# Attention followed by a max-out MoE on one core: the second product by Strassen's scheme in blocks of 512 tokens

## The chip, the core and the metric

The kernel runs on one core of one Trainium2 chip, alone. The metric is the device time of one execution in microseconds (us), lower is better. Before the change: 363.46 us, median of 3 runs (362.85 to 363.61).

## What is computed

Eight batches, eight heads, 1152 keys of 64 elements; the queries are averaged in pairs, so each head has 576 queries. The heads' outputs side by side are 4608 tokens `x` of 512 elements, which go through a two-branch max-out layer:

```
q_pool = q.reshape(B, H, S // 2, 2, D).mean(axis=3)
attn   = softmax(q_pool @ k.T / sqrt(D))
x      = (attn @ v).transpose(0, 2, 1, 3).reshape(4608, 512)
out    = np.maximum(x @ w1, x @ w2) @ w_out          # w1, w2: 512 x 1024; w_out: 1024 x 512
```

The kernel uses max(h1, h2) = h2 + relu(h1 - h2): with `wd = w1 - w2` and `w21 = w2 @ w_out`, formed once, out = x @ w21 + relu(x @ wd) @ w_out. So a token costs a first product (512 x 1024) and a second product whose contraction is 512 + 1024 = 1536 long, in 12 chunks of 128.

## The kernel before, in words

Two heads are one of 32 pairs. Their scores lie as one stream of 336 groups of 512 columns; a group is one `S` in the order of TensorE (PE): `scores` (L678) writes it into one of the PSUM buffers `sps0..2` (three for the first 21 groups, then two), and ScalarE (ACT) takes the exponential from there into `et` (L685). `av_jobs` (the `a` units: L589, and L601 for the 64 rows left over) multiply `et` by `v`, VectorE (DVE) divides by the sums (L611, L615, L619), and `xT`, the transposed tokens, is made by DMA (`xtrans`) or PE (`xtrans_pe`). GpSimd (POOL) casts k, v and q (L457, L496, L490). DVE also transposes q in 32 x 32 squares (L546).

The first product is `h_pairs` (`H` units, L877; later `h_jobs`, `h`, L850), evacuated by DVE with a relu into `gT` (L887, L861). The second product is `p_pair` (`P`): two tiles of 128 tokens, all 512 output columns, 12 chunks; one DVE copy (L919) frees its two banks, and `store_pair` sends the tokens out. The last tokens go tile by tile (`p_job`, `p`, L940). Here, 15 pairs make 3840 tokens and 6 tiles the other 768. `P`, `H` and `S` units use half the PE array's rows per matmul, two matmuls side by side (`duo`); `a`, `h`, `p` units use all 128 rows. Each `duo` job goes through its chunks twice (`turn` 0 and 1, the row halves exchanged), and the first unit of turn 1 carries `fence=True`: it waits until the unit before it on the same banks is complete.

Nothing is scheduled at run time. `pe_order` is a fixed string: one letter for each unit, `S` for a score group and a digit for the PSUM bank that a job runs in; the lists `jobs_of` say which job comes next in a bank. `dve_order`, `act_order`, `pool_order` and `sp_order` do the same for the other queues. `Plan` derives the waits from keys read and written (`r`, `w`): an instruction waits for the last writer of every key that it reads, and for the last writer and all readers, stores too, of every key that it writes.

Of the kernel before, what the change touches and what calls it, by code (L numbers as in the profile page):

```python
# [6 lines left out]
FP32 = mybir.dt.float32  # L7
# [12 lines left out]
class Plan:  # L20
# [26 lines left out]
    def lane(self, o):  # L47
# [3 lines left out]
        if o["eng"] == "POOL":  # L51
            return {"kb": "k", "wd": "d"}.get(key[:2], key[0])
# [5 lines left out]
        return {"qt": "T", "w2": "W", "wo": "W", "gd": "G"}.get(key[:2], "Q")  # L58
# [234 lines left out]
def bass_funnel_attn__then__act_maxout2_kernel(  # L293
# [23 lines left out]
    RING = 1024  # L317
    assert D == 64 and S == NT * P and QU == NT and C == H * D and E == 512
# [13 lines left out]
    with outer:  # L332
# [23 lines left out]
        xT = sbuf([P, NC_, NTOK], BF16, "xT")  # L356
# [6 lines left out]
        w2b = xT[:, :, 512:1536]  # L363
        w2T = xT[:, :, 1536:2560].rearrange("p c (f x) -> p c f x", x=P)
        w2f = xT[:, :, 2560:4608].bitcast(FP32)
# [3 lines left out]
        osb = [osb2[:, s, :] for s in range(4)]  # L369

# [132 lines left out]
        def dve(fn, r, w):  # L503
            op("DVE", fn, r=r, w=w)
# [216 lines left out]
        def xtrans(i):  # L721
            b, ct = divmod(i, NHP)
            for j, z, n0, n in spots(b):
                n1 = n0 + n * (z - j)
                op("SP", lambda e, j=j, z=z, n=n, n0=n0, n1=n1: e.dma_start_transpose(
                    xT[:, ct, n0:n1].rearrange("p (j x) -> p j x", x=n),
# [3 lines left out]
        def xtrans_pe(i):  # L730
# [9 lines left out]
            def evac(m):  # L740
                mb = fb[m][:, :].bitcast(BF16)
                op("DVE", lambda e: e.tensor_copy(xT[:, ct, b * SQ:b * SQ + SQ], mb[:, 0:SQ]),  # L742
                   r=[f"f{m}"], w=xkeys(ct, b * SQ, b * SQ + SQ) + [f"f{m}"],
                   after=under(ct, b * SQ, b * SQ + SQ))
            return Job([unit(xneed(i, 0) + xneed(i, 1) + ["ident"], go)], evac)

        def xkeys(ct, n0, n1):
            return [f"xT.{ct}.{j}" for j in range(n0 // HP, n1 // HP)]
# [40 lines left out]
        ocount = [0]  # L789
# [52 lines left out]
        def h_jobs(nb, tail):  # L842
# [24 lines left out]
        def h_pairs(nb):  # L867
# [4 lines left out]
            for f0 in range(0, NF, 2):  # L872
                def part(ct, turn, f0=f0):
                    def pair(e, m):
                        for k in range(2):
# [3 lines left out]
                                xT[z, ct, n0:n1], start=(turn == 0 and ct == 0),  # L879
# [13 lines left out]
        def p_pair(lo):  # L893

            def part(j, turn):
                if j < NC_:
                    r = [f"w21{j}"] + xkeys(j, lo, lo + 2 * P)
                else:
                    r = [f"wo{j - NC_}"] + [f"gT.{g}.{j - NC_}" for g in gkeys(lo, lo + 2 * P)]

                def pair(e, m):
                    for k in range(2):
                        z = rows(turn ^ k)
                        n = lo + k * P
                        if j < NC_:
                            lhs, rhs = xT[z, j, n:n + P], w21[z, j, :]
                        else:
                            c = n % RING
                            lhs, rhs = gT[z, j - NC_, c:c + P], wo[z, j - NC_, :]
                        last = e.matmul(fb[m + k][:, :], lhs, rhs, start=(turn == 0 and j == 0),  # L910
                                        stop=(turn == 1 and j == NC_ + NF - 1))
                    return last
                return duo(r, pair, turn == 1 and j == 0)

            def evac(m):
                ocount[0] += ocount[0] % 2
                o = ocount[0] % 4
                ocount[0] += 2
                dve(lambda e: e.tensor_copy(  # L919
                    osb2[:, o:o + 2, :], wide[m // 2][:, :, :]), [f"f{m}", f"f{m + 1}"],  # L920
# [330 lines left out]
```

## Time and profile before

| | |
|---|---|
| median of 3 runs | 363.46 us |
| span of the profiled execution, first to last instruction | 361.7 us |
| PE / ACT / DVE / POOL busy | 355.0 / 313.3 / 243.1 / 124.5 us |
| granted PE clock, mean | 0.999 |
| first and last exponential start | 6.4 and 329.8 us |
| chain that ended last: PE / ACT | 93% / 5% |

The profile shows one execution. A matmul's row gives its duration from first to last element; two that follow each other overlap, so what counts is the distance of their starts. "x8" in a row of the timeline merges eight instructions in a row.

### The profile page before, as it was taken

To read this page: it belongs to the slowest core of one execution; us is meant where nothing else is said; L and a number is where in the kernel's file an instruction comes from. 1 tells how busy PE (TensorE), PEld (TensorE's weight loads), DVE (VectorE), ACT (ScalarE), POOL (GpSimd) and SP (SyncE) were. 2 spreads that over 40 slices of the span, in tenths; PEclk is the share of its full clock that TensorE was granted. 3 is DMA by queue.
4 is the path that set the end of the run, shared out by engine and by line. 5 is a ranking of instruction groups with operands and counts; after the bars stand their busy time and mean duration, and the time that the engine had idled before them with its cause. 6 is when DMAs were issued, how large, how long until landed. Compare 5 with 4: busy or idle time off the path is not lost.

```text
span 361.7 us, 13398 instructions
## 1 busy us (share of the span) xinstructions
PE 355.0 (98%) x5973; PEld 222.1 (61%) x5973; DVE 243.1 (67%) x528; ACT 313.3 (87%) x355; POOL 124.5 (34%) x111
## 2 busy tenths in 40 slices
PE   8899999999999999999999999999999999999996
PEld 6666655566564666657575666666666565656753
DVE  3676787877589777866876687595977747625411
ACT  5999989989999999998999999989999988994221
POOL 1248967333055324452242426261234440010000
PEclk9999999999999999999999999999999999999999
DMA  7999999999959998997999999998999560805215
GB/s 239 408 394 398 402 286 296 244 286 344 246 123 242 284 302 235 251 256 179 285 309 184 269 277 284 305 251 202 243 215 269 169 153 15 198 16 87 52 30 147
DMA packets 77789, 84.76 MB, mean 234 GB/s; under 512 B 50080, under 2 KB 50848, under 8 KB 77728
## 3 DMA queue, kind: packets, MB, share of 16 engines
q1 hardware_dynamic: 77168, 83.09, 87.6%
q8 instruction: 47, 0.77, 0.9%
q10 hardware_dynamic: 560, 0.79, 0.6%
q14 instruction: 14, 0.11, 0.1%
HBM read 62.91 MB, written 9.44 MB: 200 GB/s over the span
## 4 chain that ended last, share of the span: by engine, by line
PE 93%; ACT 5%; issue 0%; DVE 0%; DVEq 0%
PE sps L678 20%; PE sps L589 13%; PE sps L910 12%; PE fb L910 10%; PE sps L877 9%; PE fb L589 7%; PE fb L877 7%; ACT et L685 5%; PE sps L940 3%; PE sps L601 2%; PE fb L802 2%; PE fb L940 1%; PE sps L850 1%; PE fb L601 1%; PE fb L850 1%; PE fb L411 1%
## 5 line engine op out<-in xcount | busy, mean ns | idle before, releaser
L685 ACT ACTIVATE et<-sps 128x1024 bf16<-128x1024 f32 (+1 forms) x336 | 305.2, 1009 | 20.5 <-PE sps L678 19.3
L678 PE MATMUL sps<-qpT,kT 64*128 64x256 bf16 (+7 forms) x1162 | 119.8, 284 | 1.7 <-DVE qpT L536 0.7
L546 DVE STREAM_TRANSPOSE qpT<-qp 32x288 bf16<-32x288 bf16 x216 | 101.4, 469 | 4.5
L678 PEld LDWEIGHTS sps<-qpT,kT 64*128 64x128 bf16 x1162 | 47.3, 94 | 51.1 <-ACT et L685 19.9
L490 POOL TENSOR_TENSOR qp<-qraw 128x576 bf16<-128x576 f32 x30 | 42.2, 1406 | 83.1 <-DVE qpT L546 58.6
L496 POOL TENSOR_SCALAR vE<-vraw 128x1152 bf16<-128x1152 f32 x32 | 36.8, 1152 | 62.8 <-DMA vraw<-in_v_dram 48.1
L589 PE MATMUL sps<-vE,et 128*128 128x65 bf16 x1440 | 51.2, 193 | 0.6 <-issue 0.4
L589 PEld LDWEIGHTS sps<-vE,et 128*128 128x128 bf16 x1440 | 46.0, 97 | 6.9 <-issue 5.4
L457 POOL TENSOR_SCALAR kbf<-kraw 128x1152 bf16<-128x1152 f32 x31 | 35.6, 1151 | 42.2 <-DMA kraw<-in_k_dram 29.6
L877 PE MATMUL sps<-xT,wd 64*128 64x512 bf16 (+3 forms) x368 | 42.8, 326 | 0.1
L910 PE MATMUL sps<-wo,stage 64*128 64x512 bf16 x256 | 37.5, 377 | 0.0
L877 PE MATMUL fb<-xT,wd 64*128 64x512 bf16 (+3 forms) x272 | 33.0, 334 | 0.1
L887 DVE TENSOR_SCALAR stage<-sps 128x1024 bf16<-128x1024 f32 (+3 forms) x23 | 22.3, 969 | 15.4 <-PE sps L877 15.2
L910 PE MATMUL fb<-wo,stage 64*128 64x512 bf16 x224 | 32.5, 377 | 0.0
L589 PE MATMUL fb<-vE,et 128*128 128x65 bf16 x864 | 30.5, 193 | 0.0
L589 PEld LDWEIGHTS fb<-vE,et 128*128 128x128 bf16 x864 | 27.5, 97 | 4.2 <-issue 3.2
L887 DVE TENSOR_SCALAR stage<-fb 128x1024 bf16<-128x1024 f32 (+3 forms) x17 | 17.0, 999 | 10.4 <-PE fb L877 10.1
L877 PEld LDWEIGHTS sps<-xT,wd 64*128 64x128 bf16 x368 | 15.6, 94 | 12.0 <-DVE xT L742 0.8
L611 DVE RECIPROCAL rcs<-sps 128x5 f32<-128x5 f32 (+1 forms) x40 | 7.3, 183 | 19.4 <-PE sps L589 18.7
L919 DVE COPY stage<-sps 128x1024 f32<-128x1024 f32 x8 | 9.8, 1224 | 13.8 <-PE sps L910 13.8
L910 PE MATMUL sps<-w,xT 64*128 64x512 bf16 x128 | 18.6, 377 | 0.0
L910 PE MATMUL fb<-w,xT 64*128 64x512 bf16 x112 | 18.1, 377 | 0.0
(94 smaller groups left out, 286.3 us busy)
## 6 DMA issues: line engine op xcount, KB each, us to landing
vraw<-in_v_dram SPq DMA_DIRECT2D x32, 576.0 KB, 6.3
kraw<-in_k_dram SPq DMA_DIRECT2D x31, 576.0 KB, 6.4
qraw<-in_q_dram SPq DMA_DIRECT2D x31, 576.0 KB, 6.0
out_dram<-stage SPq DMA_DIRECT2D x21, 256.0 KB, 5.4
out_dram<-stage SPq DMA_DIRECT2D x23, 128.0 KB, 3.0
xT<-in_moe_w_dram SPq DMA_DIRECT2D x4, 512.0 KB, 10.7
stage<-in_moe_w_out_dram SPq DMA_DIRECT2D x4, 512.0 KB, 13.7
stage<-in_moe_w_dram SPq DMA_DIRECT2D x4, 512.0 KB, 13.4
```

The lines of the kernel that those rows point to most:

```text
L457: op("POOL", lambda g: g.tensor_scalar(kbf[s][:, :, :, :].rearrange("p t h d -> p h t d"), kraw[r][:, :, :, :], 1.0, 1.0, ALU.mult, ALU.mu ...
L490: op("POOL", lambda g: g.tensor_tensor(qpf[s][:, :, :], qraw[r][:, :, 0, :], qraw[r][:, :, 1, :], ALU.add), r=[f"qraw{r}"], w=[f"qp{s}.0", ...
L496: op("POOL", lambda g: g.tensor_scalar(vE[r][:, :, :, 0:D].rearrange("p t h d -> p h t d"), vraw[r][:, :, :, :], 1.0, 1.0, ALU.mult, ALU.m ...
L546: op("DVE", lambda e: e.transpose(view[dst:dst + 32, :, 32 * pb:32 * pb + 32], qpf[s][src:src + 32, :, 32 * db:32 * db + 32]), r=[f"qp{s}. ...
L589: last = e.matmul(fb[m][:, sb * 66:sb * 66 + 65], et[:, a:a + P], vE[vs][:, t, half, 0:65], start=(t == 0), stop=(t == NT - 1))
L601: last = e.matmul(fb[m][rows(half), NCH * 66:NCH * 66 + 65], et[:, a:a + NB], vE[vs][:, t, half, 0:65], start=(t == 0), stop=(t == NT - 1))
L678: last = e.matmul(sps[r][:, h, col:col + hi - lo], kT[i % 3][rows(h), t, :], qpT[i % 3][rows(h), lo:hi], start=True, stop=True)
L685: op("ACT", lambda e: e.activation(et2[:, :, c:c + z - a], sps[r][:, :, a - g * W:z - g * W], EXP, scale=scale), r=[f"s{r}"], w=keys + ([f ...
L877: last = e.matmul(fb[m + k][:, 0:size], wd[z, ct, (f0 + k) * P:(f0 + k + 1) * P], xT[z, ct, n0:n1], start=(turn == 0 and ct == 0), stop=(t ...
L887: dve(lambda e: e.tensor_scalar_max(gT[:, f0:f0 + 2, g0:g0 + size], wide[m // 2][:, :, 0:size], 0.0), [f"f{m}", f"f{m + 1}"], w + [f"f{m}" ...
L910: last = e.matmul(fb[m + k][:, :], lhs, rhs, start=(turn == 0 and j == 0), stop=(turn == 1 and j == NC_ + NF - 1))
L940: return e.matmul(fb[m][:, 0:c1 - c0], lhs, rhs[:, c0:c1], start=(j == 0), stop=(j == NC_ + NF - 1))
```

## The change

Blocks of 512 tokens replace the pairs of 256 in the second product. The block's tokens are split in two sets of tiles (`row` 0 and 1), the contraction in two halves (`k`) and the 512 output columns in two halves (`c`), and Strassen's scheme in Winograd's form makes the four results from 7 products instead of 8. Each product is 6 chunks x 2 tiles x 2 row halves, 24 matmuls of 256 columns; so 168 matmuls of 256 columns for 512 tokens, where two `P` had 96 of 512. A block has four jobs (`P0.0` to `P0.3`) of two, two, two and one products, each with its own fence and its own evacuation.

New operations: `t_sums`, four sums of weight blocks, made once on DVE in two parts each; `s_sums`, four sums of token blocks for each block, in two parts each (`at` 0: from `xT`, 512 elements a partition; `at` 1: from `gT`, 1024), all on POOL but the parts `at` 1 of sums 1 and 3, which are on DVE; and the evacuations `end1` to `end4`, one copy and six adds of PSUM and `part`, in place of two copies. `xT` becomes a ring of 2304 tokens. Eight blocks make 4096 tokens, the last 512 go as four `p` tiles, and the output buffer of a `p` tile follows from its number, no longer from a counter.

Letters behind the first 208 PE units, the lists of jobs and the orders of the other queues are new.

```diff
-        xT = sbuf([P, NC_, NTOK], BF16, "xT")
+        xT = sbuf([P, NC_, XRING], BF16, "xT")              # XRING = NTOK // 2
+        extra = sbuf([P, NC_ * XRING], BF16, "extra")
...
+        tw = extra[:, 0:4 * KT * HE].rearrange("p (n t e) -> p n t e", n=4, t=KT)
...
+        sx = [t.rearrange("p (t j x) -> p t j x", t=KT, j=2) for t in (
+            extra[:, 4 * KT * HE:5 * KT * HE], extra[:, 5 * KT * HE:6 * KT * HE], spare16[:, 0:KT * HE])]
...
-        def p_pair(lo):
...
-                return duo(r, pair, turn == 1 and j == 0)
-            def evac(m):
...
-                dve(lambda e: e.tensor_copy(
-                    osb2[:, o:o + 2, :], wide[m // 2][:, :, :]), [f"f{m}", f"f{m + 1}"],
-                    [f"osb{o}", f"osb{o + 1}", f"f{m}", f"f{m + 1}"])
-                store_pair(lo, o)
+        def t_sums(n, at):
...
+            op("DVE", lambda g: g.tensor_tensor(t(n), one, two, ALU.subtract),
+               r=r, w=[f"tw{n}.{at}"], after=[f"w2f{c}" for c in range(NC_)])
...
+        def s_sums(lo, n, at):
+            t0, t1 = ((0, 2), (2, KT))[at]
+            a11, a12, a21, a22 = ((0, 0), (0, 1), (1, 0), (1, 1))
+            one, two, alu, dst = ((a21, a22, ALU.add, 0), (0, a11, ALU.subtract, 1),
+                                  (a11, a21, ALU.subtract, 2), (a12, 1, ALU.subtract, 1))[n]
...
+                op("DVE" if at and n % 2 else "POOL", lambda g, js=js, view=view: g.tensor_tensor(
+                    sx[dst][:, t0:t1, js, :], view(one, v1), view(two, v2), alu),
+                    r=r1 + r2, w=[f"sx{dst}.{at}"], after=[f"w2f{NC_ - 1}", f"wof{NC_ - 1}"], fence=True)
...
+        def p_block(lo):
...
+                def pair(e, m):
+                    for t in ts:                                # two chunks a unit
+                        for k in range(2):
+                            z = rows(turn ^ k)
+                            lhs, rhs = left(a, k, t)[0], right(b, t)[0]
+                            last = e.matmul(
+                                fb[m + k][:, x * HE:x * HE + HE], lhs[z, :], rhs[z, :],
+                                start=opening and t == 0, stop=closing and t == KT - 1)
...
+            def end1(m):
+                dve(lambda e: e.tensor_copy(part[:, :, 0, :], bank(m, X0)), [f"f{m}", f"f{m + 1}"], ["p1"])
+                add(m, part[:, :, 1, :], part[:, :, 0, :], bank(m, X1), ["p1"], ["u2"], True)
+            def end2(m):
+                add(m, otile(0)[:, :, 0:HE], part[:, :, 0, :], bank(m, X0), ["p1"], ["osb0.0", "osb2.0"],
+                    after=["osb0", "osb2"])
+                add(m, part[:, :, 0, :], part[:, :, 1, :], bank(m, X1), ["u2"], ["p1", "u3"], True)
+            def end3(m):
+                add(m, part[:, :, 1, :], part[:, :, 1, :], bank(m, X0), ["u2"], ["u2"])
+                add(m, otile(1).rearrange("p j (n e) -> p j n e", n=2),
+                    part[:, :, 0:1, :].to_broadcast([P, 2, 2, HE]),
+                    wide[m // 2].rearrange("p j (n e) -> p j n e", n=2), ["u3"], ["osb1", "osb3"], True)
+            def end4(m):
+                add(m, otile(0)[:, :, HE:E], part[:, :, 1, :], bank(m, X0), ["u2"], ["osb0", "osb2"], True)
+                for j in range(2):
+                    store_pair(lo + 2 * j * P, 2 * j)
...
+            return [Job(stage_units(ps), end) for ps, end in (
+                (((X0, A11, B11), (X1, 1, 1)), end1),
+                (((X0, A12, B21), (X1, 2, 2)), end2),
+                (((X0, 0, 0), (X1, A22, 3)), end3),
+                (((X0, 1, B22),), end4))]
...
             def evac_part(m):
-                o = ocount[0] % 4
-                ocount[0] += 1
+                o = lo // P % 4
...
-            "0S67676SS6677S0000S6S0066S660S6666S000S006S666S60S0000SS1111S666S0000S000S066S66S0000SS11011S"
+            "767SS666S66S0000S00S600S60S000S7777SS66666S000S00S60S0060S666S666S6000S000S066S66S660S66S1000S6S1011"
```

Three places show how the orders moved. In the names, `sps` and `fb` are PSUM, `vE,et` marks an `a` unit, `qpT,kT` a score group, `xT,wd` an `H` or `h` unit; `extra` and `stage` hold the sums.

PE, about the middle of the program, two heads' `a` jobs. Before:

```order
L601 MATMUL sps<-vE,et 64x65 x18
L589 MATMUL sps<-vE,et 128x65 x18
L678 MATMUL sps<-qpT,kT 128x384 x2
L678 MATMUL sps<-qpT,kT 128x128 x2
L678 MATMUL sps<-qpT,kT 128x448 x2
L678 MATMUL sps<-qpT,kT 128x64 x2
L589 MATMUL sps<-vE,et 128x65 x54
```

And in the changed kernel:

```order
L599 MATMUL sps<-vE,et 128x65 x9
L688 MATMUL sps<-qpT,kT 128x384 x2
L688 MATMUL sps<-qpT,kT 128x128 x2
L599 MATMUL sps<-vE,et 128x65 x27
L688 MATMUL sps<-qpT,kT 128x448 x2
L688 MATMUL sps<-qpT,kT 128x64 x2
L611 MATMUL sps<-vE,et 64x65 x18
L688 MATMUL sps<-qpT,kT 128x512 x2
L599 MATMUL sps<-vE,et 128x65 x18
```

A job of `a` units stood in two runs between the score groups, and stands in four now. Over the whole order the `a` units stand in 75 runs before and 102 now; the places where one unit uses the array in another row or column split than the unit before it are 218 before and 270 now.

PE again, the block of 128 tokens in the first product, before (8 matmuls of turn 0, a score group, 8 of turn 1):

```order
L877 MATMUL sps<-xT,wd 128x128 x8
L678 MATMUL sps<-qpT,kT 128x320 x2
L678 MATMUL sps<-qpT,kT 128x192 x2
L910 MATMUL fb<-wo,stage 128x512 x2
L877 MATMUL sps<-xT,wd 128x128 x8
```

And now:

```order
L888 MATMUL sps<-xT,wd 128x128 x16
L688 MATMUL sps<-qpT,kT 128x192 x2
L688 MATMUL sps<-qpT,kT 128x320 x2
L888 MATMUL fb<-xT,wd 128x128 x16
L888 MATMUL sps<-xT,wd 128x512 x2
```

A row "x16" holds the fenced unit right behind the unit that it waits for. Fenced units are 57 before and 74 now; with nothing in between, 1 before and 12 now.

DVE, the end of the program, with the semaphores that each waits for (`d_o0` and `d_z0`: the stores of output buffer 0 by SP and by ACT). Before:

```order
L861 TENSOR_SCALAR stage<-sps 128x128
L861 TENSOR_SCALAR stage<-sps 128x256 [waits sem_PE]
L1192 TENSOR_LOAD flag [waits sem_DVE]
L967 COPY stage<-fb 128x512 [waits sem_d_o3,sem_PE]
L967 COPY stage<-sps 128x512 [waits sem_d_o0,sem_PE]
L954 COPY stage<-sps 128x128 [waits sem_PE,sem_d_z0,sem_d_o0]
```

And now:

```order
L1015 TENSOR_TENSOR stage<-stage,sps 128x2x512 [waits sem_d_o3,sem_DVE]
L1015 TENSOR_TENSOR stage<-stage,sps 128x2x256 [waits sem_PE]
L1334 TENSOR_LOAD flag [waits sem_DVE]
L1085 COPY stage<-sps 128x512 [waits sem_PE,sem_d_o0]
L1085 COPY stage<-fb 128x512 [waits sem_PE,sem_d_o2]
L1073 COPY stage<-sps 128x128 [waits sem_PE,sem_d_z3,sem_d_o3]
```

The last tile is made in two parts, 384 columns copied out and stored by way of ACT, and then 128 columns copied by DVE. Before, the two parts lie in buffers 3 and 0; now both lie in buffer 3.

More of the change, by code (lines that the diff above doesn't have):

```diff
@@ L891, in h_pairs @@
             return jobs
-        def p_pair(lo):
[L895 to L899, printed above, removed]
-                def pair(e, m):
[L902 to L911, printed above, removed]
-                    return last
-                return duo(r, pair, turn == 1 and j == 0)
-            def evac(m):
-                ocount[0] += ocount[0] % 2
-                o = ocount[0] % 4
-                ocount[0] += 2
-                dve(lambda e: e.tensor_copy(
-                    osb2[:, o:o + 2, :], wide[m // 2][:, :, :]), [f"f{m}", f"f{m + 1}"],
-                    [f"osb{o}", f"osb{o + 1}", f"f{m}", f"f{m + 1}"])
-                store_pair(lo, o)
-            return Job([part(j, turn) for turn in range(2) for j in range(NC_ + NF)], evac)
@@ new lines, in tiles, with akeys, ablocks @@
+        def tiles(lo, row):
+            return [lo + (2 * j + row) * P for j in range(2)]
+        def akeys(lo, row, k, at):
+            ns = tiles(lo, row)
+            if at == 0:
+                return [key for n in ns for c in range(2) for key in xkeys(2 * k + c, n, n + P)]
+            return [f"gT.{n % RING // P}.{4 * k + f}" for n in ns for f in range(4)]
+        def ablocks(lo, row, k, at):
+            src, w, size = ((xT, 2, XRING), (gT, 4, RING))[at]
+            full = src[:, k * w:k * w + w, :]
+            a = lo % size
+            if a + 4 * P <= size:
+                return [(slice(0, 2), full[:, :, a:a + 4 * P].rearrange("p t (j r x) -> p t j r x", r=2, x=P)[
+                    :, :, :, row, :])]
+            return [(slice(j, j + 1), full[:, :, n % size:n % size + P].unsqueeze(2))
+                    for j, n in enumerate(tiles(lo, row))]
@@ L1074, in chores, with fed @@
                     later(f"x{i}", [f"a{i}"] + over(i), lambda i=i: xtrans(i))
+            ready = [f"wc{n}.{ct}" for n, ct in W_CASTS] + [f"wd{ct}.{half}" for ct, half in W_DIFFS]
+            for n in range(4):
+                for at in range(2):
+                    later(f"t{n}.{at}", ready + ["W0", "W2"][:2 - 2 * at] + [f"t{m}.{at}" for m in range(n)],
+                          lambda n=n, at=at: t_sums(n, at))
+            units = sorted({int(name[1:]) for name in count if name[0] == "P"})
+            for lo, back in zip(units, [None] + units):
+                def fed(row, k, lo=lo):
+                    return [f"H{nb}.{f}" if f"H{nb}" in count else f"h{nb}.{f + g}"
+                            for nb, (n0, n1) in enumerate(hblocks)
+                            if any(n0 < n + P and n < n1 for n in tiles(lo, row))
+                            for f in range(4 * k, 4 * k + 4, 2) for g in ((0,) if f"H{nb}" in count else (0, 1))]
+                here = [f"x{i}" for i in range(lo // SQ * NHP, ((lo + 4 * P - 1) // SQ + 1) * NHP)]
+                for n, dst in enumerate((0, 1, 2, 1)):
+                    for at in range(2):
+                        own = (fed(1, 0) + fed(1, 1), fed(0, 0), fed(0, 0) + fed(1, 0), fed(0, 1))[n]
+                        need = ready + (own if at else here) + [f"s{lo}.{m}.{at}" for m in ((), (0,), (), (1,))[n]]
+                        if n == 3:
+                            need.append(f"P{lo}.0")
+                        elif back is not None:
+                            need.append(f"P{back}.{(2, 3, 1)[n]}")
+                        later(f"s{lo}.{n}.{at}", need, lambda lo=lo, n=n, at=at: s_sums(lo, n, at))
         def more_banks(groups):
```

174 lines of the change are left out of this document (119 added, 55 removed), and 33 rows, old and new, of the table jobs_of.

## The prediction

> **What bounds the kernel now.** I read the page first, then the waits of PE, then one wide window, then the timeline of PE for prices, and last the end of the program.
>
> ```profile
> span 361.7 us, 13398 instructions
> PE 355.0 (98%) x5973; PEld 222.1 (61%) x5973; DVE 243.1 (67%) x528; ACT 313.3 (87%) x355; POOL 124.5 (34%) x111
> L685 ACT ACTIVATE et<-sps 128x1024 bf16<-128x1024 f32 (+1 forms) x336 | 305.2, 1009 | 20.5 <-PE sps L678 19.3
> ...
> PE fb L411 <- DVE warm L396: 1.1, 1, 1.1
> PE sps L678 <- DVE qpT L536: 0.7, 2, 0.4
> PE sps L678 <- ACT et L685: 0.4, 1, 0.4
> PE sps L678 <- DVE kT L566: 0.4, 2, 0.3
> PE sps L589 <- issue: 0.4, 1, 0.4
> PE sps L589 <- ACT et L685: 0.2, 1, 0.2
> ...
> 60.00:300.00 240.00, 239.75 (x4183) 148.28 (x4179) 177.65 (x387) 225.75 (x250) 88.99 (x73) 1.00 1.00 246
> ```
>
> PE is busy for 98% of the span; all its waits come to 3.2 us, nearly all of them in the start-up. In the window from 60 to 300 us (columns: PE, weight loads, DVE, ACT, POOL) PE is busy 239.75 of 240 us and DVE 177.65, 74%. ACT's 336 exponentials sat idle 20.5 us in all. So PE's own work sets the time, and a change is worth what it adds to or takes from PE's row of starts, plus what it makes PE wait for, plus what lies behind PE's last matmul.
>
> **Prices on PE**, from the timeline (start, duration, count), where the distance of two starts is the price:
>
> ```profile
> 203.99 0.61 PE L877 MATMUL sps<-xT,wd 64*128 64x256 bf16 x8
> 204.43 0.38 PE L910 MATMUL fb<-w,xT 64*128 64x512 bf16 x2
> ...
> 204.87 0.60 PE L910 MATMUL fb<-w,xT 64*128 64x512 bf16 x4
> 205.30 0.38 PE L678 MATMUL sps<-qpT,kT 64*128 64x256 bf16 x4
> ...
> 209.02 0.38 PE L678 MATMUL sps<-qpT,kT 64*128 64x512 bf16 x2
> 209.24 0.81 PE L910 MATMUL fb<-wo,stage 64*128 64x512 bf16 x6
> 209.89 0.39 PE L678 MATMUL sps<-qpT,kT 64*128 64x512 bf16 x2
> 210.21 0.47 PE L601 MATMUL sps<-vE,et 128*64 128x65 bf16 x18
> ...
> 110.35 0.34 PE L877 MATMUL fb<-xT,wd 64*128 64x128 bf16 x6
> ...
> 110.74 0.63 PE L877 MATMUL fb<-xT,wd 64*128 64x128 bf16 x8
> ...
> 351.79 0.81 PE L940 MATMUL sps<-wo,stage 128*128 128x512 bf16 x3
> ```
>
> *Columns.* Two matmuls of 64 rows run side by side. Eight of 256 columns start at 203.99 and the next unit at 204.43: 0.110 us a couple. Four of 512 columns take 204.87 to 205.30: 0.215 a couple. A full-row matmul of 512 takes the same: three last 0.81, one 0.38, so 0.215 each. Before, 15 pairs x 24 couples x 0.215 = 77.4 us and the two tiles that move into blocks 2 x 12 x 0.215 = 5.2: 82.6. After, 8 blocks x 84 couples x 0.110 = 73.9. **-8.7 us**, all on PE's path. No row has the weights changing with each 256-column couple in a `P` unit; the `H` unit of the first row does just that, so I take its price.
>
> *Changes of the array's split.* A score couple of 512 columns followed by a unit of the same split takes 0.22 (209.02 to 209.24); followed by an `a` unit, 0.32 (209.89 to 210.21): 0.10 us for the change. The order has 270 of them for 218, since the `a` jobs are cut in 102 runs for 75. 52 x 0.10 = **+5.2**. Nothing hides it: it is PE itself.
>
> *Fences.* Six matmuls of 64x128 take 0.34, so a couple adds 0.06 and eight should take 0.40; the eight at 110.74, which hold a fence with nothing in between, took 0.63. The one adjacent fence costs 0.23; the order now has 12. 11 x 0.23 = **+2.5**.
>
> **The end.** The timeline's last rows, and what the last stores took (size, us to landing):
>
> ```profile
> 358.12 0.48 ACT L950 COPY stage<-sps 128x384 f32<-128x384 f32 x1 [0.65 <-PE sps L940]
> 358.63 1.37 ACTq L819 DMA_DIRECT2D out_dram<-stage  x2
> 358.75 0.29 DVE L954 COPY stage<-sps 128x128 f32<-128x128 f32 x1 [2.67 <-PE sps L940]
> ...
> out_dram<-stage ACTq DMA_DIRECT2D x1, 96.0 KB, 2.6
> ...
> out_dram<-stage ACTq DMA_DIRECT2D x1, 32.0 KB, 2.5
> ```
>
> Before, DVE's last copy (358.75) runs beside the store of the 384 columns and its own store lands 2.5 us later, at the span's end. Now both parts lie in one buffer and the copy waits for both stores of the first part: issued at 358.63, landed 2.6 later at 361.2, copy 0.29, and the last store starts at about 361.5 in place of 359.1. **+2.4 us**; behind it only the last store waits, and nothing covers it. Between the ends: 0 if the store landed at once, 2.6 if the issue is late too; I take what the rows give.
>
> **What DVE and POOL get.**
>
> ```profile
> L919 DVE COPY stage<-sps 128x1024 f32<-128x1024 f32 x8 | 9.8, 1224 | 13.8 <-PE sps L910 13.8
> L967 DVE COPY stage<-sps 128x512 f32<-128x512 f32 x1 | 0.7, 692 | 1.8 <-PE sps L940 1.8
> L619 DVE TENSOR_TENSOR xnat<-sps,rcs 128x256 bf16<-128x256 f32 x40 | 16.6, 423 | 1.1
> L484 DVE TENSOR_TENSOR qp<-qraw 128x576 bf16<-128x576 f32 x1 | 0.7, 748 | 0.0
> L784 DVE COPY xT<-fb 128x1024 bf16<-128x1024 bf16 x3 | 2.1, 688 | 1.8 <-PE fb L778 1.8
> L490 POOL TENSOR_TENSOR qp<-qraw 128x576 bf16<-128x576 f32 x30 | 42.2, 1406 | 83.1 <-DVE qpT L546 58.6 <-DMA qraw<-in_q_dram 24.4
> L770 POOL TENSOR_TENSOR wd<-stage,xT 128x512 bf16<-128x512 f32 x8 | 10.0, 1272 | 0.1
> ```
>
> An evacuation of 512 elements takes 0.69, of 1024 1.22; a second source changes nothing (256 elements: 0.42). A block now takes six of 512 and one of 1024, 5.4 us: 8 x 5.4 - 15 x 1.22 = +24.5. The 16 sums of 1024 on DVE have no row: above, 1.04 ns an element as the fp32 sum of 576 (0.75), 1.21 us each; below, 0.69, what 1024 bf16 elements take in a copy. Both inputs and the output are bf16, so I take 0.69: 11 (to 19.4). The weight sums likewise 4.4 (to 7.6). Together +40 us; with seven eighths of it in the window above, DVE goes from 74% to 89% there.
>
> The Trainium skill says ("VectorE: DVE Perf Modes", section "Mode 2×_1P — pack two bf16 into one 32-bit read") that a sum of two tensors reaches two results a cycle when all are 16-bit with step one, and one otherwise. That is the lower end; no row here shows a bf16 sum, and by the upper one the forecast would be 0.9 us later, a tenth of 8.4 (below).
>
> What PE feels of DVE has no row. Below, it is nothing: at 74% PE lost no measurable time in the window. Above, a quarter of the added 40: each block has four evacuations for two, each holds its banks 0.7 to 1.9 us where a copy held them 1.2, two pairs of banks serve all jobs while scores run, and DVE waits in its queue for POOL's 2.3 us sum before sum 1, with q transposes and relus queued behind. DVE's idle share falls from 26% to 11%. I take a tenth, nearer the lower end because that is where the window stands: **+4** (0 to 10).
>
> POOL gains 8 x (4 x 1.27 + 2 x 2.34) = 78 us (2.1 ns an element between its two rows), 124 to 203, 55%. Its sums stand between the casts of k, v and q; the casts run ahead of use in three buffers, so I price that at nothing. If that cover goes, q is late, then DVE's transposes, then scores. The ring is written again 2304 tokens later, half a program: nothing. ACT has its 20.5 us of idle time: nothing. As many bytes are stored as before.
>
> **The sum.** -8.7 + 5.2 + 2.5 + 2.4 + 4 = +5.4. Against the profiled span, 361.7 becomes 367.1; the median lies 1.8 above it, and I keep that: 368.9.
>
> **Rivals.**
>
> *DVE's sums and POOL shut each other out: 374.* The only DVE sums with two SBUF inputs so far never ran beside POOL:
>
> ```profile
> 7.81 0.48 DVE L484 TENSOR_TENSOR qp<-qraw 128x320 bf16<-128x320 f32 x1
> 12.69 0.75 DVE L484 TENSOR_TENSOR qp<-qraw 128x576 bf16<-128x576 f32 x1
> ...
> 10.77 1.15 POOL L457 TENSOR_SCALAR kbf<-kraw 128x1152 bf16<-128x1152 f32 x1 [3.67 <-DMA kraw<-in_k_dram]
> 14.36 1.15 POOL L496 TENSOR_SCALAR vE<-vraw 128x1152 bf16<-128x1152 f32 x1 [2.44 <-DMA vraw<-in_v_dram]
> ```
>
> If each of the 24 new ones (16 and 8) must let POOL's instruction finish, it waits in 55% of cases for half of 1.15 to 2.3 us, some 0.8: 24 x 0.55 x 0.8 = 10.6 us on a DVE that has 11% left. Half of it on PE: +5. From about 5 us on DVE it decides. For it: POOL doubles its share. Against: no row. The Trainium skill states this rule ("SBUF — State Buffer", section "🔬 SBUF: two separate sides"): such a DVE instruction and a GpSimd one that reads SBUF hold the shared port in turn, and the later one blocks. No run here shows it.
>
> *DVE keeps up: 364.9.* The fourth term is 0. For it: the order puts other PE work behind nearly every evacuation, as before. Still +0.4%.
>
> *The new order loses less than the old: 361.7.* All 3.2 us of PE's waits go, and DVE adds none: 364.9 - 3.2. It decides from 2.2 us on. Against: these waits lie in the start-up, whose units are the same.
>
> *The change is given back exactly*, 363.5: 1.4 us recovered so, and no DVE wait.
>
> **How the numbers follow.** A run of this kernel tells 0.2% from no change: 362.7 to 364.2. Forecast, with 1 to 8 us from DVE, 365.9 to 372.9: 0.48. Shut out: 0.20. DVE keeps up: 0.12. Less loss: 0.12, since a whole order is new and its waits can't be read from the old trace. Given back: 0.08. Faster 0.12, same 0.08, slower 0.80. The range takes in the exact give-back, the case where DVE keeps up and most of the shut-out one, 363.2 to 377; the forecast alone is 365.9 to 372.9.
>
> **What would show it.** Right: 1344 matmuls of 64x256 about 0.110 apart a couple; DVE's last copy idle some 2.4 us more, ended by a DMA; PE's waits on DVE some 4 us, DVE over 75%. Wrong: PE's starts farther apart in `P` units; DVE's sums of 1024 far above 0.69; a PE that waits for ACT or a late q.

## The result, and the profile after

The changed kernel takes 390.5 us (median of 4 runs, 387.3 to 394.2) against 363.15 before: 1.073 times as long, 95% interval 1.068 to 1.077. The forecast was 368.9, its range up to 377: the sign is right, the size wrong by 21.6 us. A run more than 1.5% above the fastest of its kernel counts as slow (here the one of 394.2): it stays in the medians and is left out of every ratio, and without it the changed kernel's median is 389.8. The other three runs spread over 3.8 us, those of the kernel before over less than 1 in this comparison (362.7 to 363.6); that limits what small edits can show below.

From the profile page of the changed kernel, the span, the busy line and the line of the exponentials:

```profile
span 389.8 us, 14744 instructions
PE 359.7 (92%) x6569; PEld 251.4 (64%) x6573; DVE 287.9 (74%) x593; ACT 313.1 (80%) x353; POOL 200.1 (51%) x163
L695 ACT ACTIVATE et<-sps 128x1024 bf16<-128x1024 f32 (+1 forms) x336 | 306.2, 1009 | 37.8 <-PE sps L688 36.7
```

The wide window (columns: PE, weight loads, DVE, ACT, POOL, granted clock):

```profile
60.00:300.00 240.00, 219.43 (x4135) 151.91 (x4133) 194.19 (x399) 207.96 (x229) 140.17 (x109) 0.96 0.99 240
```

PE was busy for 239.75 of these 240 us before; now it stands idle for 20.6 of them, at a clock of 0.96. PE's longest waits, and one of POOL:

```profile
PE sps L990 <- DVE extra L958: 10.8, 2, 6.3
PE sps L888 <- DVE stage L898: 3.8, 2, 3.0
PE fb L990 <- DVE extra L958: 1.8, 1, 1.8
PE sps L990 <- DVE extra L920: 1.6, 1, 1.6
...
POOL kbf L467 <- DMA kT<-kbf: 57.3, 18, 6.5
```

The same wait of POOL in the kernel before:

```profile
POOL kbf L457 <- DMA kT<-kbf: 12.5, 5, 4.8
```

PE waits for DVE's sums (L958), relus (L898) and weights' sums (L920); and POOL, which had nothing to do with PE's end before, waits 57 us for DMA transposes of k. The last matmuls and DVE's last copy, after, and then the last matmuls before:

```profile
383.21 0.61 PE L1060 MATMUL sps<-wo,stage 128*128 128x128 bf16 x8
...
387.39 0.29 DVE L1073 COPY stage<-sps 128x128 f32<-128x128 f32 x1 [4.00 <-DMA out_dram<-stage]
```

```profile
358.00 0.61 PE L940 MATMUL sps<-wo,stage 128*128 128x128 bf16 x8
```

PE ends at 383.8 (358.6 before) and was busy for 359.7 us (355.0), so up to its end it was idle for 24.1 us (3.6). The span's 28.1 us are 20.5 us more idle time of PE, 4.7 us more busy time, and 2.9 us more behind its end (6.0 for 3.1). The busy time holds a loss that is no work. Four stretches behind waits of PE of 3.0, 4.4, 1.8 and 6.3 us:

```profile
70.00:73.00 3.00, 3.00 (x24) 1.28 (x22) 2.56 (x6) 1.55 (x2) 2.89 (x3) 0.60 1.03 394
139.00:144.00 5.00, 4.53 (x42) 2.88 (x44) 1.76 (x7) 1.73 (x2) 2.27 (x2) 0.50 1.08 334
178.00:182.00 4.00, 4.00 (x79) 2.98 (x75) 3.89 (x9) 3.25 (x4) 1.29 (x2) 1.00 1.29 189
263.00:267.00 4.00, 3.76 (x34) 2.37 (x36) 2.77 (x7) 1.57 (x2) 1.26 (x2) 0.50 0.98 171
```

Behind the three long waits the granted clock (last column but two) is 0.50 to 0.60, behind the short one 1.00. Of 3.00, 4.53 and 3.76 us busy, 1.2, 2.3 and 1.9 are lost so (busy time times the missing share of the clock), an estimate of 5.4 us in all. Without them PE's busy time changed by -0.7 us; the three PE terms of the prediction sum to -1.0.

The longest wait, in the timeline of POOL, DVE and PE:

```profile
249.47 2.12 POOL L958 TENSOR_TENSOR stage<-stage 128x1024 bf16<-128x1024 bf16 x1
258.05 1.15 POOL L467 TENSOR_SCALAR kbf<-kraw 128x1152 bf16<-128x1152 f32 x1 [6.47 <-DMA kT<-kbf]
259.17 2.11 POOL L958 TENSOR_TENSOR extra<-stage 128x1024 bf16<-128x1024 bf16 x1
261.31 1.87 DVE L958 TENSOR_TENSOR extra<-extra,stage 128x1024 bf16<-128x1024 bf16 x1 [5.59 <-POOL extra L958]
263.24 1.03 PE L990 MATMUL sps<-extra 64*128 64x256 bf16 x8 [6.33 <-DVE extra L958]
```

POOL is done with one sum at 251.6. Next in its queue is the cast of a k pair. It writes `kbf`, of which there are two, and the DMA transpose that reads that buffer lands 6.5 us later. Only then come the cast, the next Strassen sum (259.17), DVE's sum 1, which reads what POOL's sum wrote, and PE's product. Nothing that PE needed at 263 was computed by the cast; it stood ahead.

### The profile page after: what moved, and what is told of

The parts are those of the page before. It is cut to its first block, busy times and chain, and to the rows that moved or that the text cites. A ratio compares the mean times of both kernels' runs of the same rounds, so it can differ in the third digit from the quotient of the medians.

```text
span 389.8 us, 14744 instructions
## 1 busy us (share of the span) xinstructions
PE 359.7 (92%) x6569; PEld 251.4 (64%) x6573; DVE 287.9 (74%) x593; ACT 313.1 (80%) x353; POOL 200.1 (51%) x163
## 4 chain that ended last, share of the span: by engine, by line
PE 52%; issue 17%; POOL 11%; DVE 11%; ACT 5%; DMA 2%; SPq 1%; ACTq 0%; POOLq 0%; DVEq 0%
PE sps L688 11%; PE sps L990 8%; PE sps L599 7%; PE fb L990 6%; ACT et L695 5%; PE sps L888 5%; PE fb L599 4%; PE fb L888 3%; POOL extra L958 3%; DVE qpT L556 3%; POOL qp L500 3%; DVE extra L920 2%; POOL vE L506 2%; PE fb L812 1%; POOL kbf L467 1%
## 5 line engine op out<-in xcount | busy, mean ns | idle before, releaser
L467 POOL TENSOR_SCALAR kbf<-kraw 128x1152 bf16<-128x1152 f32 x31 | 36.6, 1180 | 65.4 <-DMA kT<-kbf 57.3
L500 POOL TENSOR_TENSOR qp<-qraw 128x576 bf16<-128x576 f32 x30 | 45.1, 1505 | 15.2 <-DMA qraw<-in_q_dram 8.8
L599 PE MATMUL sps<-vE,et 128*128 128x65 bf16 x1296 | 47.8, 193 | 0.4 <-ACT et L695 0.2
L599 PEld LDWEIGHTS sps<-vE,et 128*128 128x128 bf16 x1296 | 42.0, 97 | 8.8 <-issue 6.8
L599 PE MATMUL fb<-vE,et 128*128 128x65 bf16 x1008 | 38.1, 193 | 0.0
L599 PEld LDWEIGHTS fb<-vE,et 128*128 128x128 bf16 x1008 | 32.8, 97 | 7.8 <-issue 6.8
L990 PE MATMUL sps<-extra 64*128 64x256 bf16 x216 | 16.8, 285 | 12.5 <-DVE extra L958 10.8
L898 DVE TENSOR_SCALAR stage<-sps 128x1024 bf16<-128x1024 f32 (+3 forms) x21 | 21.6, 1029 | 7.8 <-PE sps L888 7.5
L1015 DVE TENSOR_TENSOR stage<-stage,sps 128x512 f32<-128x512 f32 (+1 forms) x25 | 19.1, 768 | 9.5 <-PE sps L990 9.1
L958 POOL TENSOR_TENSOR stage<-stage 128x1024 bf16<-128x1024 bf16 x8 | 17.0, 2122 | 14.5 <-DVE stage L898 11.2
L958 POOL TENSOR_TENSOR extra<-xT,extra 128x512 bf16<-128x512 bf16 (+1 forms) x9 | 9.4, 1047 | 22.6 <-PE sps L990 19.6
L990 PEld LDWEIGHTS sps<-extra 64*128 64x128 bf16 x216 | 10.2, 99 | 16.3 <-DVE extra L958 11.3
L898 DVE TENSOR_SCALAR stage<-fb 128x1024 bf16<-128x1024 f32 (+3 forms) x19 | 17.6, 926 | 3.3 <-PE fb L888 3.0
L1015 DVE TENSOR_TENSOR stage<-stage,fb 128x512 f32<-128x512 f32 (+1 forms) x23 | 17.8, 776 | 2.4 <-PE fb L990 2.0
```

The costliest lines, as they stand in the source:

```text
L467: op("POOL", lambda g: g.tensor_scalar(kbf[s][:, :, :, :].rearrange("p t h d -> p h t d"), kraw[r][:, :, :, :], 1.0, 1.0, ALU.mult, ALU.mu ...
L500: op("POOL", lambda g: g.tensor_tensor(qpf[s][:, :, :], qraw[r][:, :, 0, :], qraw[r][:, :, 1, :], ALU.add), r=[f"qraw{r}"], w=[f"qp{s}.0", ...
L599: last = e.matmul(fb[m][:, sb * 66:sb * 66 + 65], et[:, a:a + P], vE[vs][:, t, half, 0:65], start=(t == 0), stop=(t == NT - 1))
L898: dve(lambda e: e.tensor_scalar_max(gT[:, f0:f0 + 2, g0:g0 + size], wide[m // 2][:, :, 0:size], 0.0), [f"f{m}", f"f{m + 1}"], w + [f"f{m}" ...
L958: op("DVE" if at and n % 2 else "POOL", lambda g, js=js, view=view: g.tensor_tensor(sx[dst][:, t0:t1, js, :], view(one, v1), view(two, v2) ...
L990: last = e.matmul(fb[m + k][:, x * HE:x * HE + HE], lhs[z, :], rhs[z, :], start=opening and t == 0, stop=closing and t == KT - 1)
```

## The experiments

Two theories for the missing 21.6 us. **A, place in POOL's queue:** sums stand behind k casts that wait for a DMA. **B, shut out,** the prediction's rival: DVE's two-input sums and POOL's instructions exclude each other. B has rows too: DVE's sum above took 1.87 us where others of its line took 0.68, and POOL's q cast has a mean of 1505 ns for 1406 before.

**A third buffer for the cast k**, in `cast_k`, `ktrans` and `ktrans_pe`; the room comes from the half of the `qp` buffers that nothing reads.

```
-        kbf = [sbuf([P, NT, 2, D], BF16, f"kbf{s}") for s in range(2)]
+        kbf = [sbuf([P, NT, 2, D], BF16, f"kbf{s}") for s in range(3)]
...
-            s, r = i % 2, i % 3
+            s, r = i % 3, i % 3
...
-                    later(f"ck{i}", [f"lk{i}", f"ck{i - 1}"] + old("k", i, 2), lambda i=i: cast_k(i))
+                    later(f"ck{i}", [f"lk{i}", f"ck{i - 1}"] + old("k", i, 3), lambda i=i: cast_k(i))
```

> The changed kernel (390.5 us median) with three buffers for the cast k in place of two, so that POOL's cast of k pair i waits for the DMA transpose of pair i-3, not i-2; nothing else changes, POOL's order is the same. Theory A (POOL's in-order queue: its k casts wait 57 us for the kT transposes, with Strassen sums queued behind them, DVE's sum 1 behind those and PE behind that): POOL's idle time on the kT transposes falls under 15 us, the stalls of PE at 139, 178 and 263 us (4.6, 2.0 and 6.5 us) go, and the time falls by 13 to 18 us, to 372 to 377. Rival B (DVE's sums with two SBUF inputs and POOL shut each other out): POOL's waits fall as well, but the time stays within 4 us, 386 to 390.

376.2 us (375.1 to 377.2), ratio 1.038 (1.035 to 1.041): 14.3 us less (13.6 among the runs that the ratios use), as A has it. Its waits (its lines are one lower):

```profile
POOL kbf L466 <- DMA kT<-kbf: 5.4, 2, 4.3
...
PE sps L887 <- DVE stage L897: 2.8, 2, 2.0
PE sps L989 <- DVE extra L919: 1.3, 1, 1.3
PE fb L989 <- DVE extra L957: 1.3, 3, 0.4
```

POOL's wait went from 57.3 to 5.4 us, and the stalls at 139, 178 and 263 us went with it.

**One input for DVE's 24 sums.**

```
-            op("DVE", lambda g: g.tensor_tensor(t(n), one, two, ALU.subtract),
+            op("DVE", lambda g: g.tensor_reduce(t(n), one.unsqueeze(3), AX.X, ALU.max),
...
+                (lambda g, js=js, view=view: g.tensor_reduce(
+                    sx[dst][:, t0:t1, js, :], view(one, v1).unsqueeze(4), AX.X, ALU.max)) if at and n % 2 else
```

> The changed kernel with each of DVE's 24 sums of 1024 bf16 elements (8 of the weights, 16 of the blocks) made a reduction over an axis of length one: one SBUF input in place of two, same output, same place, about 1.2 us each. The second input is left out of the computation. Rival B (shut out): POOL's casts return to 1.41 (q), 1.15 (k) and 1.15 us (v) at most, from up to 1.90, 1.59 and 1.59; the 24 take one duration; the time falls by 9 us or more, to 381 or less. Theory A (POOL's queue): the durations become uniform too, but the stalls of PE at 139, 178 and 263 us stay; the time moves by less than 4 us.

390.6 us (388.3 to 392.1): no change, as A has it. The groups of DVE and POOL:

```profile
L958 DVE TENSOR_REDUCE extra<-stage 128x1024 bf16<-128x1024 bf16 x8 | 9.7, 1214 | 0.1
L958 DVE TENSOR_REDUCE extra<-extra 128x1024 bf16<-128x1024 bf16 x8 | 9.7, 1211 | 13.7 <-POOL extra L960 13.7
L500 POOL TENSOR_TENSOR qp<-qraw 128x576 bf16<-128x576 f32 x30 | 42.2, 1405 | 11.6 <-DMA qraw<-in_q_dram 8.7 <-DVE qpT L556 2.9
```

Without a second input DVE's block sums all take 1.21 us, and POOL's q cast is back at 1405 ns, as the exclusion has it. But to take it away brings nothing that shows while POOL's queue holds the sums up: DVE's idle time ahead of them, ended by POOL, is 13.7 us. The test is not quite clean. A one-input sum takes longer than a two-input one that POOL leaves alone (0.68), so DVE's 16 block sums took 19.4 us here, for 15.4 in the changed kernel.

**POOL's sums almost without work.**

```
+            X = P if lo == 0 or (at and n % 2) else 8
...
-                    sx[dst][:, t0:t1, js, :], view(one, v1), view(two, v2), alu),
+                    sx[dst][:, t0:t1, js, 0:X], view(one, v1)[:, :, :, 0:X],
+                    view(two, v2)[:, :, :, 0:X], alu),
```

> The changed kernel with POOL's Strassen sums cut to 8 of 128 columns from the second block on (the rest of the operands is left as the first block's), DVE's sums untouched; POOL's order and all waits are the same. POOL's own load falls by some 65 us. Theory A (position in the queue): a sum stands behind the same waiting cast, so the stalls at 139, 178 and 263 us lose only the 1 to 2 us of the sum itself; the time falls by 4 to 10 us, to 380 to 386. Rival C (POOL's load itself, 78 us): the stalls nearly all go and the time is 366 to 372.

385.05 us (381.1 to 385.9): 5.4 less (4.8 among the runs that the ratios use), within A's range and far from that of C, POOL's load itself. The longest stall, in the timeline:

```profile
171.31 1.15 POOL L467 TENSOR_SCALAR kbf<-kraw 128x1152 bf16<-128x1152 f32 x1 [6.64 <-DMA kT<-kbf]
172.43 1.40 POOL L500 TENSOR_TENSOR qp<-qraw 128x576 bf16<-128x576 f32 x1
173.78 0.30 POOL L959 TENSOR_TENSOR extra<-stage 128x64 bf16<-128x64 bf16 x1
...
174.12 1.62 DVE L959 TENSOR_TENSOR extra<-extra,stage 128x1024 bf16<-128x1024 bf16 x1 [5.99 <-POOL extra L959]
...
175.79 0.82 PE L992 MATMUL fb<-extra 64*128 64x256 bf16 x6 [6.48 <-DVE extra L959]
```

A sum of 0.30 us still holds PE up for 6.5: what costs is where it stands.

**POOL's order at three places**, with the two buffers of the changed kernel (`k`, `q`, `v` are casts, `r` and `s` sums):

```
-kqrvs
+rskqv
...
-kqs
+skq
...
-ks
+sk
```

> The changed kernel, two buffers of cast k as it has them, with only POOL's order altered at three places: the Strassen sums that stood behind a waiting k cast at 130, 172 and 258 us now stand ahead of it. Theory A (position in POOL's queue): each sum runs in the time in which POOL stood idle, the k casts start when they did, the stalls of PE at 139, 178 and 263 us (4.6, 2.0 and 6.5 us) go, and the time falls by 10 to 15 us, to 376 to 381. Rival D (the third buffer helped because k itself came earlier, to scores): the time stays within 3 us of 390.5.

380.8 us (376.8 to 382.7), ratio 1.046 (1.039 to 1.052): 9.7 less (9.4 among the runs that the ratios use), at the upper end of A's 376 to 381. The three stalls are gone, and one of 3.3 us came up at 293, behind another waiting k cast. POOL's k casts wait even longer for their DMA here; what changed is what stands behind them:

```profile
POOL kbf L467 <- DMA kT<-kbf: 79.5, 21, 6.7
```

So it is the order; more memory was one way round it.

**The end.** The last 128 columns in another output buffer, alone and with the third `kbf`:

```
-                o = lo // P % 4
+                o = (lo // P + (c0 > 0)) % 4
```

> The changed kernel with the last 128 columns of the last tile in another output buffer, so that DVE's last copy no longer waits for the store of the first 384 columns (4.0 us idle in the profile). Term of the prediction: 2.4 us less, 388.1. Rival: the store issues in one queue hold it up anyway, 390.5.

> Three buffers of cast k (376.2 us by itself) and the last 128 columns in an output buffer of their own. The prediction's term for the end: 2.4 us less, 373.8; the trace of the changed kernel has 6.0 us from PE's last matmul to the end of the span and 3.2 before the change, so 2.8 less, 373.4. Rival: the two effects overlap and it stays at 376.

385.2 us (383.5 to 392.7) alone, 377.2 (375.7 to 378.9) with the third buffer: the runs spread wider than the effect, so the times don't settle it. The profiles do. From PE's end to the span's end it is 5.8 to 6.0 us in the five kernels so far without this edit and 4.2 to 4.5 in all with it: 1.5 of the 2.9 us. DVE's last copy in the second kernel still waits, now for the store of an earlier tile:

```profile
374.42 0.29 DVE L1072 COPY stage<-sps 128x128 f32<-128x128 f32 x1 [2.52 <-DMA out_dram<-stage]
```

**What is left between 60 and 90 us.** The second of these kernels, in that stretch:

```profile
60.00:90.00 30.00, 24.84 (x410) 14.64 (x406) 27.81 (x50) 23.57 (x27) 23.30 (x17) 0.89 1.14 312
```

DVE is 93% busy and POOL 78%. In this kernel the weights' sums were replaced by fills with a constant; then, besides, the blocks' sums were cut as above, DVE's too:

```
-            op("DVE", lambda g: g.tensor_tensor(t(n), one, two, ALU.subtract),
+            op("DVE", lambda g: g.memset(t(n), 0.01),
```

> As the run before, and DVE's 8 sums of weights (9.8 us between 56 and 86 us) replaced by fills with a constant of the same size: the weights' sums are left out of the computation. Theory A' (what is left after POOL's queue is DVE at 94% between 60 and 90 us): the stalls of PE at 61, 69, 79 and 88 us (1.0, 2.2, 1.5 and 0.9 us) and the lower clock behind them (0.91) go, 6 to 7 us less, 367. Rival: DVE's q transposes and evacuations alone keep PE waiting there, and it is within 2 us of 373.5.

> As the run before, and all Strassen sums of the blocks, POOL's and DVE's, cut to 8 of 128 columns from the second block on. What is left is PE's own work and the four evacuations of each block. The prediction's own terms without the end and without DVE give 363.1 - 8.7 + 5.2 + 2.5 = 362.1. If the columns, split changes and fences are as predicted, 361 to 364; if a term of PE is wrong, or the evacuations of a block hold PE up by themselves, 365 or more.

371.9 us (371.3 to 372.5) and 371.1 (370.2 to 372.0). Both miss their first number, and the second does not tell which of its two causes it was. A fill of 1024 takes 0.91 us, so DVE's eight instructions fell only from 9.3 to 5.6 us, and yet 5 us went. What the fills also don't have is an SBUF input. Next, the order of DVE alone (`B` is a weights' sum, `T` a q transpose, `S` a block's sum, a digit an evacuation):

```
-BTT6
+B6TT
...
-TTB6
+6TTB
...
-TTTBB10B
+BBBTTT10
...
-B6S6
+B66S
...
-TTTTT7S
+TTTSTT7
...
-7T76S
+S7T76
```

> Three buffers of cast k and the own output buffer (376 to 377 us), with DVE's order altered at six places: the relu evacuations that PE waits for at 62 and 70 us stand ahead of the weight sum and the q transposes that stood before them, four weight sums ahead of three transposes (PE waits for one at 81 us), the block's second evacuation ahead of a sum at 89 us, and two sums of the blocks ahead of transposes at 217 and 291 us. Nothing is added or removed. Theory A' (place in DVE's queue, at 94% between 60 and 90 us): the stalls of PE at 62, 70, 81 and 90 us (1.1, 2.5, 1.2 and 0.9 us) and the half clock from 69 to 75 us (3 us lost) shrink, 4 to 7 us less, 370 to 373. Rival (DVE is simply full there, so that what goes ahead pushes another wait behind it): within 2 us of 376.5.

375.8 us (374.1 to 380.0, ratio 1.029 to 1.039): the rival. The relus' waits went, and PE now waits for a weights' sum:

```profile
73.62 2.62 POOL L957 TENSOR_TENSOR extra<-stage 128x1024 bf16<-128x1024 bf16 x1
74.18 2.34 DVE L919 TENSOR_TENSOR extra<-w 128x512 bf16<-128x512 bf16 x1
...
77.03 0.39 PE L989 MATMUL sps<-extra 64*128 64x256 bf16 x4 [2.60 <-DVE extra L919]
```

A sum of 512 elements took 2.34 us; DVE's other two of that size next to it took 0.42 and 0.62. It ended at 76.52, 0.28 us behind POOL's sum, which itself took 2.62 us where the median of its like is 2.12. That is B. So the weights' sums were cut to 8 of 256 columns (the products read plain blocks of the weights in their place), with two inputs and then with one, and at last left whole with one:

```
-            op("DVE", lambda g: g.tensor_tensor(t(n), one, two, ALU.subtract),
+            op("DVE", lambda g: g.tensor_tensor(t(n)[:, :, 0:8], one[:, :, 0:8], two[:, :, 0:8], ALU.subtract),
...
+            op("DVE", lambda g: g.tensor_reduce(t(n)[:, :, 0:8], one[:, :, 0:8].unsqueeze(3), AX.X, ALU.max),
...
+            op("DVE", lambda g: g.tensor_reduce(t(n), one.unsqueeze(3), AX.X, ALU.max),
```

> Three buffers of cast k and the own output buffer (376 to 377 us), with DVE's 8 sums of weights cut to 8 of 256 columns; the products take plain blocks of the weights in their place, so the weights' sums are left out. DVE sheds some 8 us between 56 and 86 us, where the fills of an earlier run still took 0.91 us each. If DVE full between 60 and 90 us is what holds PE there (6.5 us of stalls and 2 to 3.4 us by the half clock): 9 us less, 367 to 369. Rival (the relus of the first block and the q transposes hold PE there by themselves): no better than the 371.9 of the run with fills.

> As e11 (372.5: three buffers, own output buffer, weights' sums cut to 8 columns), but the cut sums read one input in place of two. If the exclusion by POOL is what the cut sums spend their time on: they take some 0.1 us each instead of 0.56 to 1.04, DVE's busy time from 60 to 90 us falls from 29.2 by 4 us or more, PE's stalls there (5.3 us) shrink to 2 or less, and the time is 367 to 369.5. Rival (DVE's transposes and evacuations alone fill that stretch): the durations fall, but the time stays at 371 to 373.

> As e6 (377.2: three buffers, own output buffer), with the 8 weights' sums whole but with one input (1.22 us for 1024, 0.67 for 512, 7.6 us in all; the second input is left out of the computation). With the exclusion they take 9 to 11 us, so DVE gets 2 to 3 us back and POOL its 5: if the exclusion counts for PE here, 373 to 375; if not, 376 to 378.

372.5 us (370.6 to 373.5), 370.75 (369.1 to 371.0) and 372.4 (371.7 to 372.9). The groups of these sums in the first, the second and the third:

```profile
L919 DVE TENSOR_TENSOR extra<-wo,extra 128x32 bf16<-128x32 bf16 x2 | 2.7, 1356 | 0.1
L919 DVE TENSOR_TENSOR extra<-w,extra 128x16 bf16<-128x16 bf16 x2 | 1.4, 686 | 0.0
```

```profile
L919 DVE TENSOR_REDUCE extra<-wo 128x32 bf16<-128x32 bf16 x4 | 0.7, 184 | 0.1
L919 DVE TENSOR_REDUCE extra<-w 128x16 bf16<-128x16 bf16 x4 | 0.6, 157 | 0.1
```

```profile
L919 DVE TENSOR_REDUCE extra<-wo 128x1024 bf16<-128x1024 bf16 x4 | 4.9, 1217 | 0.1
L919 DVE TENSOR_REDUCE extra<-w 128x512 bf16<-128x512 bf16 x4 | 2.7, 674 | 0.1
```

The two rows of the first kernel are the slower half of its sums; the other half has means of 0.63 and 0.26 us. Its timeline shows what the time goes to:

```profile
75.24 1.43 POOL L499 TENSOR_TENSOR qp<-qraw 128x576 bf16<-128x576 f32 x1
75.24 0.15 DVE L919 TENSOR_TENSOR extra<-w 128x16 bf16<-128x16 bf16 x1
...
75.49 1.20 DVE L919 TENSOR_TENSOR extra<-w,extra 128x16 bf16<-128x16 bf16 x1
```

Of two sums of 16 elements, both with two inputs, one took 0.15 us and one 1.20, and the second ended 0.02 us behind POOL's instruction. So it is not the second input by itself that takes long; nearly all of the 1.36 us is the wait for POOL. The first kernel, whose sums are nearly free of work but still wait, is no faster than the fills, as its rival has it. The third is the cleanest test: the sums at full size without the exclusion (7.6 us on DVE for 9.3) are 4.8 us faster than 377.2 (ratio 1.023 to 1.028, for 1.034 to 1.043), more than expected. PE's longest wait there, for a relu, went from 2.3 to 1.5 us, and its stretch keeps the full clock, where the mean was 0.89 (PE was busy for nearly 6 us at half clock from 70 to 76 us, an estimate of 3 us lost). So a large part of the 4.8 us is the half clock, not the sums' own waits:

```profile
60.00:90.00 30.00, 25.71 (x481) 16.28 (x477) 29.20 (x61) 26.44 (x30) 22.16 (x18) 1.00 1.16 305
```

The second missed its 367 to 369.5 by 1.3 us and lies nearer to its rival: DVE's busy time in this stretch fell by 2.7 us (26.5 for 29.2), not by 4, and PE is still not busy for 2.7 us of the 30. With the weights' sums cut as in the first, and the blocks' sums cut from the second block on:

> As the run before, and all Strassen sums of the blocks, POOL's and DVE's, cut to 8 of 128 columns from the second block on: PE's own work, its fences and the four evacuations of each block. Prediction's terms without DVE: 362.1, and 1 us more at the end, as the trace of the earlier run has it (4.2 us behind PE's last matmul for 3.2): 363. If 363 to 366, the terms of PE stand and all the rest was waiting; if it stays at 370 or more, evacuations alone hold PE up.

369.6 us (368.8 to 373.7), between the two cases named. PE's busy time is 354.5 us at a clock of 1.00, for 355.0 before: its own work is close to what was predicted. Its end is at 363.1 for 358.6; its idle time up to there is 8.6 us for 3.6, so 5.0 us of waiting are left. The cut sums still take 14.0 us on DVE, for 24.6 whole, so this is not a kernel without sums.

**The fences**, with the score group ahead of each of the 12 adjacent ones moved between the job's two halves; one of the 12 places:

```
-000S66666666S0
+0006666S6666S0
```

> As the run before, and in PE's order the score group that precedes each of the 12 adjacent fences moved behind one half, to stand between the two halves (up to four units later). The prediction's term, 11 to 12 fences of 0.23 us: 2.5 us less. Rival: the scores come later to ACT by up to 1.7 us twelve times and PE waits for ACT's exponentials instead: no change, or slower.

374.85 us (372.7 to 378.4), ratio 1.025 to 1.036 for 1.029 to 1.039 of the run that it builds on: not settled by the times. In its trace 3 of PE's starts inside an `H` or `P` job are more than 0.1 us late, for 14: the fences' delays went, but the time does not show it. By its median it is the fastest kernel here that does the whole computation, and 3% slower than the one before the change.

**All of the blocks' sums on POOL:**

```
-                op("DVE" if at and n % 2 else "POOL", lambda g, js=js, view=view: g.tensor_tensor(
+                op("POOL", lambda g, js=js, view=view: g.tensor_tensor(
```

> As e6 (377.2), with the blocks' 16 sums that DVE made put on POOL, each in POOL's order at the time at which DVE made it; the whole computation is done. DVE loses 16 sums (11 us, some 15 with the waits for POOL), POOL gains 16 x 2.12 = 34 us and goes to 63%. If DVE's late sums (0.6 to 0.9 us of stalls at 166, 213, 247 and 286 us) come from the exclusion and POOL keeps up: 373 to 375. If POOL's sum, three times as long as DVE's, makes the chain of a block later: 378 to 390.

386.5 us (382.65 to 388.2), 9 us slower than 377.2 and in the second range. PE now waits for POOL itself:

```profile
221.74 2.11 POOL L957 TENSOR_TENSOR extra<-extra,stage 128x1024 bf16<-128x1024 bf16 x1
...
223.91 0.50 PE L989 MATMUL fb<-extra 64*128 64x256 bf16 x6 [1.96 <-POOL extra L957]
```

These waits come to 8.7 us in the profile. Part of the loss is another thing: PE also waits 4.1 us for a weights' sum at 79 us, where it waited 1.0. DVE, even shut out at times, is the better place for sum 1: otherwise POOL, whose sum takes 2.11 us, stands last in the chain.

## Why the prediction was wrong

- **Columns, split changes, fences** (-8.7, +5.2, +2.5): right together to within a microsecond, -1.0 predicted. PE's busy time moved by -0.7 us without the half clock, and by -0.5 in the run with all sums cut; besides, the fences leave 13 gaps of some 0.07 us on PE, 0.9 us in all, which count as idle. The price of the columns is as taken, twelve matmuls of 256 in 0.66 us, 0.110 a couple:

```profile
223.67 0.82 PE L990 MATMUL fb<-extra 64*128 64x256 bf16 x12
224.33 0.38 PE L688 MATMUL sps<-qpT,kT 64*128 64x192 bf16 x4
```

  The other two are not shown singly.
- **The end** (+2.4): right, 2.9 in the profile, with the wait for the store that was forecast; another buffer takes back 1.5 of it, since the copy then waits for an earlier store.
- **POOL, "priced at nothing"**: this is the step that failed. Its reason, that the casts run ahead of use in three buffers, is true of the raw loads and of `kT`; the cast k has two. And it named the wrong victim, "q is late". No cast was late for its use (PE's waits for `qpT` and `kT` are 0.7 and 0.3 us, 0.7 and 0.4 before); the casts waited in the queue for a DMA, as they had for 12.5 us before, and what was new is that sums stood behind them and PE behind the sums. The prediction counted DVE's wait for "POOL's 2.3 us sum", not for what stands ahead of that sum. The third buffer took 14.3 us back, of which some 4.2 are the half clock at 139 and 263 us (2.3 and 1.9).
- **What PE feels of DVE** (+4, 0 to 10): the term was to hold all waits of PE; 20.5 us of idle time and 5.4 at half clock came in its place. A tenth of the added work is no price where two nearly full engines meet: in the 30 us from 60 to 90 the kernel with the third buffer and the output buffer of its own still lost 5.2 us of PE's time, besides the clock of 0.89.
- **Half clock**: no term had it. It added some 1.2 to 2.3 us to each of the three long waits.
- **Shut out** (0.20, 374): the mechanism exists, as the Trainium skill states it ("SBUF — State Buffer", section "🔬 SBUF: two separate sides": whichever comes first holds the port and the other blocks). The trace agrees: 1.36 us against 0.18, and with two inputs alike 1.20 against 0.15. The price was spread evenly, 0.8 us over 24 sums; measured, the 8 sums of the weights cost 4.8 us, which shows in the time only after POOL's queue is mended (before that, 390.6 without it and 390.5 with it). The 16 sums of the blocks are stretched too, to 15.3 us on DVE in the kernel of 377.2, where 16 of 0.69 would be 11.0, but no run takes the exclusion from them alone.
- **A bf16 sum of 1024 on DVE**, taken at 0.69 us: 0.68 where POOL leaves it alone. That is the lower end of the prediction, which "VectorE: DVE Perf Modes", section "Mode 2×_1P — pack two bf16 into one 32-bit read", of the Trainium skill gave as two results a cycle, and the trace agrees with it rather than with the upper end of 1.21. (The tenth of 8.4 us that the prediction puts on that upper end is 0.8, not 0.9.)

Of the 27.3 us, the runs give some 14 to POOL's queue (14.3 by the third buffer, 9.7 by three places of the order) and 4.8 to the exclusion at the weights' sums; 1.5 of the end shows in the profiles only. With these three mended it is 372.4, still 9.3 over the kernel before. In that profile PE's busy time is 354.8 us, 0.2 less than before, the end takes 1.2 us more, and PE is idle 8.8 us more (its end at 367.2 less 354.8, for 3.6). With all sums cut there are still 5.0 such us. How the 8.8 divide between evacuations, the blocks' sums and single late instructions, no run takes apart.

## What to carry to other kernels

New work for an in-order queue is priced by what stands ahead of it there: read which instructions of that engine wait for a DMA, how long (57 us in 18 waits here), and who waits for the work put behind them. An idle engine is free room only if nothing stands on when its new work ends. And in these traces a wait of some 2.2 us or more on PE mostly cost more than itself, since the clock came back late.

## What the runs showed of the hardware that was not expected

- Two-input DVE sums of 16 to 32 elements took up to 1.36 us in the mean of a group beside a POOL that was some three quarters busy, and 0.16 to 0.18 with one input. The other way round, beside the changed kernel's whole sums POOL's q cast took 1505 ns in the mean, and 1405 where DVE's sums read one input.
- PE's granted clock was one half behind all but one (of 2.9 us) of the waits of 2.2 us or more in these traces, and behind some of 1.5 to 2.0 us but not others. It lasted 3.4 or 6.8 us each time, and once, at a wait of 6.5 us, 10.2; part of that can lie inside the wait. The bound is left open. The Trainium skill, "TensorE: Matmul & The Clock Gate", section "🔬 Part 1: The HAM clock gate (the "warmup" mystery)", gives an idle window of about 3.4 us for the drop; here waits of 2.2 us were mostly enough, so by the traces the drop comes earlier than a reader would take from it.
